# Splitting each large cache load by partitions over two DMA queues

## Chip, core and metric

The kernel runs on one core of one Trainium2 chip. The metric is the device time in microseconds (us); lower is better. Times given for single DMA packets count from the first DMA record of a trace, some 11 us before its span starts; those of profile windows count from the start of the span.

## The reference, cut to what matters

Two attention blocks for one decoded token, side by side. Block A has 32 heads, each with its own cache of 32768 keys and 32768 values of 128 bf16 numbers. Block B is small here (a window of 4096 keys, 8 cache heads).

```python
# block A; block B is the same over a window of 4096 keys
q = (x @ wq).reshape(B, Sq, H, Dh)            # B = Sq = 1, H = 32, Dh = 128
scores = einsum("bhqd,bhkd->bhqk", q, k_cache) * Dh ** -0.5
p = softmax(scores)
o = einsum("bhqk,bhkd->bhqd", p, v_cache)
out = o.reshape(B, Sq, H * Dh) @ wo
```

A head needs 8.4 MB of keys and 8.4 MB of values, each byte once. The whole kernel reads 570 MB.

## The kernel before

SyncE issues every large load. One head's keys are one transfer, its values another: 128 partitions, 64 KB contiguous in each partition. TensorE transposes the keys and multiplies; the key buffer has three thirds of 32 KB per partition, so that the next keys can be loaded while the second half of a head's keys is in use; the value buffer holds one head.

```python
def load(self, dst, src, sem, *deps):
    self.op("sp", lambda e: e.dma_start(dst, src).then_inc(sem, 16), *deps)

def kv_src(self, which, name, g):              # head g, row p = partition p: 64 KB of one head
    ...
    return src.rearrange("s (p j) d -> p s (j d)", p=128)

def load_k(self, g, parts):
    w = HALF * DH                              # 16384 elements, 32 KB: one third of the key buffer
    src = self.kv_src("k", "A", g)[:, 0, :]
    lo = min(self.k_thirds(g))
    free = [self.free["k"][t] for t in self.k_thirds(g)]
    if parts == 1:
        self.load(self.kbuf[:, w * lo:w * lo + 2 * w], src, self.mark("k", 0), *free)
        ...
def load_v(self, g):
    self.load(self.vbuf[:, :], self.kv_src("v", "A", g)[:, 0, :], self.mark("v", 0), *self.free["v"])

# plan(): the main loop, one head per turn
for g in range(NQH):
    self.load_k(g, 1 if g < NQH - 1 else 2)
    self.load_v(g)
    self.emit_qcopy(g)
    self.emit_unit("A", g)        # transposes and scores
    self.emit_stats("A", g)       # maximum, exponential
    self.emit_PT("A", g)
    self.emit_PV("A", g)          # probabilities times values
# ... weights, output projection ...
```

Of the kernel before, what the change touches and what calls it, by code (L numbers as in the profile page):

```python
# [9 lines left out]
DH = 128  # L10
NQH = 32
STRIPS = 4
HALF = 128
NT = 4
# [38 lines left out]
class _Kernel:  # L53
# [176 lines left out]
    def alloc(self):  # L230
        nc = self.nc
        sb = nc.alloc_sbuf_tensor
        self.kbuf = sb("kbuf", [128, 3 * HALF * DH], BF16)
        self.vbuf = sb("vbuf", [128, 2 * HALF * DH], BF16)
        self.kt = [sb(f"kt{i}", [128, 1024], BF16) for i in range(NKT)]
        self.psb = sb("psb", [128, 512], BF16)
        self.ptsb = sb("ptsb", [128, 512], BF16)
        self.ident = sb("ident", [128, 128], BF16)
        self.ones = sb("ones", [128, 128], BF16)
        self.e32 = sb("e32", [128, 32], F32)  # L240
        self.spread = sb("spread", [32, 4, 128], BF16)
        self.tr = {k: sb(f"tr_{k}", [128, 32], F32) for k in ("in", "a")}
        self.rows64 = sb("rows64", [128, 64], F32)
        self.nscale = sb("nscale", [1, 128], F32)
        self.m4 = sb("m4", [1, 128], F32)
        self.pb = sb("pb", [128, 512], F32)
        self.out_sb = sb("out_sb", [128, 512], BF16)
        self.c = {}
        for name, d in self.X.items():
            HG = d["HG"]  # L250
            self.c[name] = dict(
                x=sb(f"x_{name}", [128, 4], BF16),
                oc=[sb(f"oc_{name}{i}", [128, DH + 1], F32) for i in range(2)],
                b=sb(f"b_{name}", [128, 32], F32),
                cm=sb(f"cm_{name}", [128, 32], F32),
                mr=sb(f"mr_{name}", [1, HG], F32),
                nb=sb(f"nb_{name}", [128, 2], F32),
                hot=sb(f"hot_{name}", [128, d["nb"]], F32),
                lh=sb(f"lh_{name}", [128, HG], F32),
                hsel=sb(f"hsel_{name}", [128, 64], F32),  # L260
                rinv=sb(f"rinv_{name}", [32, 1], F32),
                ob=sb(f"ob_{name}", [32, DH], BF16),
                oz=sb(f"oz_{name}", [128, 32], BF16),
            )

        self.qz = sb("qz", [128, 32 * self.X["B"]["NKVH"] + 64], BF16)
        self.qa = sb("qa", [128, NQH], BF16)
        self.qw = sb("qw", [128, 64], BF16)
        self.hw = sb("hw", [128, 32], F32)
        ps = nc.alloc_psum_tensor  # L270
        self.S = ps("psS", [128, 512], F32)
        self.T = [ps(f"psT{i}", [128, 512], F32) for i in range(NT)]
        self.PT = ps("psPT", [128, 512], F32)
        self.ACC = ps("psACC", [128, 512], F32)
        self.G = ps("psG", [128, 512], F32)
        s = nc.alloc_semaphore
        self.ksem = [s(f"ksem{i}") for i in range(2)]
        self.vsem = [s(f"vsem{i}") for i in range(2)]
        self.xsem = {n: s(f"xsem_{n}") for n in self.X}
        self.wosem = {n: [s(f"wosem_{n}{i}") for i in range(len(self.WO_CUTS[n]) - 1)] for n in self.X}  # L280
        self.outsem = {n: s(f"outsem_{n}") for n in self.X}
# [27 lines left out]
    def k_thirds(self, g):  # L309
        return (1, 0) if g % 2 == 0 else (1, 2)  # L310

    def load_k(self, g, parts):
        w = HALF * DH
        src = self.kv_src("k", "A", g)[:, 0, :]
        lo = min(self.k_thirds(g))
        free = [self.free["k"][t] for t in self.k_thirds(g)]
        if parts == 1:
            self.load(self.kbuf[:, w * lo:w * lo + 2 * w], src, self.mark("k", 0), *free)
            sem = self.mark("k", 1)
            self.op("sp", lambda e: e.sem_inc(sem, 16))  # L320
        else:
            for i, t in enumerate(self.k_thirds(g)):
                self.load(self.kbuf[:, w * t:w * t + w], src[:, w * (t - lo):w * (t - lo) + w], self.mark("k", i), *free)

    def load_v(self, g):
        self.load(self.vbuf[:, :], self.kv_src("v", "A", g)[:, 0, :], self.mark("v", 0), *self.free["v"])

    WQ_SLOT = {"B": 0, "A": 1}

# [20 lines left out]
    def plan(self):  # L350
        self.lsem = {"k": self.ksem, "v": self.vsem}
        self.fill = {w: [0, 0] for w in "kv"}
        self.free = {"k": [None] * 3, "v": [None] * 2}
        self.nbatch = 0
        self.copies = []
        self.pending = []
        self.psread = self.ptread = self.sread = self.accread = None
        self.gath = self.qcopy = self.hcopy = None
        self.constants()
        a, b = self.X["A"], self.X["B"]  # L360

        self.load_wq("B")
        self.load_b("k", 0)
        self.load_wq("A")
        self.load_b("k", 1)
        self.emit_qproj("B")
        self.emit_unit("B", 0)
        self.emit_qproj("A")
        self.emit_stats("B", 0)
        self.emit_unit("B", 1, {1: lambda: self.emit_PT("B", 0)})  # L370
        self.emit_stats("B", 1)
        for g in range(2):
            if g == 1:
                self.emit_PT("B", g)
            self.load_b("v", g)
            self.emit_PV("B", g)
        self.emit_spread("B")

        for g in range(NQH):
            self.loop = {"pe": g // 2, "dve": g // 2}  # L380
            self.load_k(g, 1 if g < NQH - 1 else 2)
            self.load_v(g)
            self.emit_qcopy(g)
            self.emit_unit("A", g)
            self.emit_stats("A", g)
            self.emit_PT("A", g)
            self.emit_PV("A", g)
        self.loop = {}
        for n in ("B", "A"):
            for part in range(len(self.WO_CUTS[n]) - 1):  # L390
                self.load_wo(n, part)
        self.emit_spread("A")
        self.emit_proj()
        for n in ("B", "A"):
            self.op("sp", lambda e, n=n: e.wait_ge(self.outsem[n], 16))
# [71 lines left out]
    def emit_unit(self, name, g, hooks={}):  # L467

        d = self.X[name]
        thirds = (g,) if name == "B" else self.k_thirds(g)  # L470
        lo = min(thirds)
        order = [(t, i, 8 * (t - lo) + st) for i, t in enumerate(thirds) for st in range(8)]
        for n, (t, i, st) in enumerate(order):
            for half in range(2):
                self.emit_T(HALF * lo + 16 * st + 8 * half, self.landed("k", g if name == "B" else i), t)
            if n % 2:
                if n // 2 in hooks:
                    hooks[n // 2]()
                self.pending.append((name, g, order[n - 1][2], n == 1, n == len(order) - 1, self.nbatch - 4))
                if len(self.pending) > 1:  # L480
                    self.emit_S(self.pending.pop(0))

    def emit_T(self, tile, landed, third):
        b = self.nbatch
        self.nbatch += 1
        T, KT = self.T[b % NT][:, :].bitcast(BF16), self.kt[b % NKT]
        src = self.kbuf[:, DH * tile:DH * tile + 1024]
        def tr(e):
            inst = None
            for k in range(8):  # L490
                inst = e.transpose(T[:, 128 * k:128 * k + 128], src[:, DH * k:DH * k + DH], self.ident[:, :])  # L491
            return inst
        o = self.op("pe", tr, landed, self.copies[b - NT] if b >= NT else self.k_ident, to="dve")
        self.copies.append(self.op("dve", lambda v: v.tensor_copy(KT[:, :], T[:, :]), o, to="pe"))  # L494
        self.free["k"][third] = o

# [77 lines left out]
    def emit_PV(self, name, g):  # L574
        d, t = self.X[name], self.c[name]
        acc = self.ACC
        pt = self.ptsb[:, :].rearrange("p (j x) -> p j x", x=128)
        if name == "A":
# [3 lines left out]
            rows = 4  # L582
        else:
            w = HALF * DH
# [4 lines left out]
            rows = 16  # L589
        def mm(e):  # L590
# [2 lines left out]
                inst = e.matmul(acc[32 * c:32 * c + rows, 0:512], lhsT=lhsT, rhs=rhs, start=begin, stop=end,  # L593
                                tile_position=(0, 32 * c), skip_group_check=True)
            return inst
        pv = self.op("pe", mm, self.landed("v", 0 if name == "A" else g), self.ptread, self.accread, to="sp")
        for i in (0, 1) if name == "A" else (g,):
            self.free["v"][i] = pv

        pv = self.emit_gather(name, g, DH, DH + 1)  # L600
        oc = t["oc"][g % 2][:, 0:DH]
        o = None
        for j in range(4):
            src, hot = acc[:, DH * j:DH * j + DH], t["hot"][:, j:j + 1]
            to = "pe" if j == 3 else "dve"
            if j == 0:
                o = self.op("dve", lambda v, src=src, hot=hot: v.tensor_scalar_mul(oc, src, hot), pv, self.gath, to=to)  # L607
# [96 lines left out]
```

## Time and profile before

| | before |
|---|---|
| time | 1329.17 us (1329.11 to 1329.23, 2 runs) |
| span of the profiled execution | 1326.8 us |
| read from HBM | 570.43 MB, 430 GB/s over the span |
| 64 KB packets, 5th / 50th / 95th percentile, after the first 160 us | 2.418 / 2.422 / 2.426 us |

The page of the kernel before: busy times, then slices (40 equal parts of the span; for DMA the mean busy tenths of the 16 DMA engines), traffic, the queues, and the chain of work that ended last.

```profile
span 1326.8 us, 28797 instructions
PE 964.5 (73%) x13436; PEld 679.5 (51%) x13436; DVE 749.8 (57%) x1345; ACT 54.8 (4%) x167; POOL 2.3 (0%) x17
...
DMA  9999999999999999999999999999999999999998
GB/s 394 431 431 438 432 433 433 437 429 433 433 435 437 433 435 431 433 433 435 437 433 435 431 433 433 431 441 433 431 435 433 431 433 441 433 431 435 433 431 344
...
q1 hardware_dynamic: 12776, 570.43, 99.6%
...
DMA 70%; PE 28%; DVE 1%; issue 0%; SPq 0%; ACT 0%
```

The DMA engines never rest, and the busiest compute engine, TensorE, works 73% of the time. The q1 line is SyncE's queue: packets, MB, and its share of the time of 16 engines. The chain of waits is 70% DMA. So the kernel is bound by its loads, and its rate hardly leaves room: it is flat at some 433 GB/s from the second slice to the last but one.

The two costliest TensorE groups of the same page, the transposes of the keys and the products with the values (line, engine, operation, tiles, shapes, count; busy us, mean ns of one; idle time before it and who ended it), and three DMA issues (size in KB, median us from issue to landing):

```profile
L491 PE MATMUL psT<-ident,kbuf 128*128 128x128 bf16 x8448 | 579.2, 234 | 176.2 <-DMA kbuf<-in_A_k_cache_dram 164.4
...
L593 PE MATMUL psACC<-vbuf,ptsb 128*4 128x512 bf16 (+1 forms) x2112 | 183.2, 523 | 23.1 <-ACT ptsb L568 21.3
...
vbuf<-in_A_v_cache_dram SPq DMA_DIRECT2D x32, 26.5
...
kbuf<-in_A_k_cache_dram SPq DMA_DIRECT2D x31, 27.8
...
x_B<-in_B_x_dram ACTq DMA_DIRECT2D x1, 1.0 KB, 12.5
```

TensorE waits 164 us for keys, the sign of a load-bound loop. A load lands 26 to 28 us after its issue although its bytes need only 19.35 us (the distance of successive completions), because it is issued early and queues behind the one before. That slack of about 7 us matters for judging issue costs.

### The profile page before, as it was taken

What the parts mean: (1) busy time and instruction counts of PE and PEld (TensorE: products, weight loads), DVE (VectorE), ACT (ScalarE), POOL (GpSimd) and SP (SyncE); (2) the same over time, 40 slices, a digit from 0 to 9 for tenths busy, and PEclk for the clock granted to TensorE, in tenths of its full rate; (3) what the DMA queues carried; (4) which work ended last, traced back from release to release, by engine and by line L of the source; (5) the groups of instructions that cost most, each with busy time, mean ns of one, the idle gap of its engine ahead of it and who ended that gap; (6) DMA issues with size and microseconds to landing.
All of it is one profiled execution on the core that took longest, in us unless ns stands there. A gap on an engine that the chain in (4) does not pass through costs nothing.

```text
span 1326.8 us, 28797 instructions
## 1 busy us (share of the span) xinstructions
PE 964.5 (73%) x13436; PEld 679.5 (51%) x13436; DVE 749.8 (57%) x1345; ACT 54.8 (4%) x167; POOL 2.3 (0%) x17
## 2 busy tenths in 40 slices
PE   3757678777667877766787777678777767877786
PEld 3544455554445555444565544456554445655453
DVE  3645466665456666545666645566654556665473
ACT  0000000000000000000000000000000000000000
POOL 0000000000000000000000000000000000000000
PEclk9877788887788888778888878888887888888798
DMA  9999999999999999999999999999999999999998
GB/s 394 431 431 438 432 433 433 437 429 433 433 435 437 433 435 431 433 433 435 437 433 435 431 433 433 431 441 433 431 435 433 431 433 441 433 431 435 433 431 344
DMA packets 13079, 570.66 MB, mean 430 GB/s; under 512 B 1540, under 2 KB 1544, under 8 KB 1928
## 3 DMA queue, kind: packets, MB, share of 16 engines
q1 hardware_dynamic: 12776, 570.43, 99.6%
q8 instruction: 12, 0.20, 0.1%
q10 hardware_dynamic: 288, 0.00, 0.0%
q14 instruction: 3, 0.02, 0.0%
HBM read 570.43 MB, written 0.00 MB: 430 GB/s over the span
## 4 chain that ended last, share of the span: by engine, by line
DMA 70%; PE 28%; DVE 1%; issue 0%; SPq 0%; ACT 0%
DMA kbuf<-in_A_k_cache_dram 65%; PE psT L491 23%; PE psS L513 4%; DMA kbuf<-in_B_k_cache_dram 3%; DMA kbuf<-in_A_wo_dram 3%; DVE kt L494 1%; PE psACC L593 0%; SPq L286 0%; DVE oc_A L609 0%; ACT psb L541 0%; DVE tr_in L530 0%; PE psPT L565 0%; ACT ptsb L568 0%; PE psPT L655 0%; PE psG L620 0%
## 5 line engine op out<-in xcount | busy, mean ns | idle before, releaser
L494 DVE COPY kt<-psT 128x1024 bf16<-128x1024 bf16 x1056 | 655.2, 684 | 245.0 <-PE psT L491 243.1
L491 PE MATMUL psT<-ident,kbuf 128*128 128x128 bf16 x8448 | 579.2, 234 | 176.2 <-DMA kbuf<-in_A_k_cache_dram 164.4
L491 PEld LDWEIGHTS psT<-ident,kbuf 128*128 128x128 bf16 x8448 | 539.7, 106 | 268.2 <-DMA kbuf<-in_A_k_cache_dram 172.5
L593 PE MATMUL psACC<-vbuf,ptsb 128*4 128x512 bf16 (+1 forms) x2112 | 183.2, 523 | 23.1 <-ACT ptsb L568 21.3
L513 PE MATMUL psS<-kt,qw 128*32 128x512 bf16 x2048 | 157.6, 385 | 15.5 <-DVE kt L494 15.5
L607 DVE TENSOR_SCALAR oc_A<-psACC,hot_A 128x128 f32<-128x128 f32 x32 | 11.2, 351 | 247.8 <-PE psG L620 247.8
L593 PEld LDWEIGHTS psACC<-vbuf,ptsb 128*4 128x4 bf16 (+1 forms) x2112 | 60.0, 110 | 136.9 <-issue 87.2
L541 ACT ACTIVATE psb<-psS,nb_A 128x512 bf16<-128x512 f32 x32 | 22.0, 687 | 1169.9 <-DVE nb_A L540 1169.9
L513 PEld LDWEIGHTS psS<-kt,qw 128*32 128x32 bf16 x2048 | 34.0, 95 | 58.0 <-DVE kt L494 31.4
L620 PE MATMUL psG<-oc_A,hw 128*32 128x128 f32 (+1 forms) x128 | 19.3, 227 | 52.3 <-DVE oc_A L609 52.3
L620 PEld LDWEIGHTS psG<-oc_A,hw 128*32 128x32 f32 x128 | 11.4, 109 | 62.4 <-DVE oc_A L609 55.0
L565 PE MATMUL psPT<-ident,psb 128*128 128x128 bf16 x136 | 17.9, 274 | 34.0 <-ACT psb L541 34.0
L609 DVE SCALAR_TENSOR_TENSOR oc_A<-psACC,hot_A,oc_A 128x128 f32<-128x128 f32 x96 | 33.7, 351 | 3.4
L530 DVE TENSOR_REDUCE tr_in<-psS 128x1 f32<-128x512 f32 x34 | 23.5, 692 | 17.1 <-PE psS L513 17.1
L565 PEld LDWEIGHTS psPT<-ident,psb 128*128 128x128 bf16 x136 | 10.0, 116 | 37.0 <-ACT psb L541 36.7
L534 PE MATMUL psACC<-rows,tr_in 128*1 128x64 f32 x64 | 8.7, 217 | 25.6 <-DVE tr_in L530 25.6
L568 ACT ACTIVATE ptsb<-psPT 128x512 bf16<-128x512 bf16 x34 | 20.3, 597 | 28.2 <-PE psPT L565 28.2
L534 PEld LDWEIGHTS psACC<-rows,tr_in 128*1 128x1 f32 x64 | 2.7, 81 | 35.1 <-DVE tr_in L530 35.1
L538 PE MATMUL psACC<-mr_A,nscale 1*128 1x1 f32 x64 | 12.1, 256 | 9.8 <-DVE mr_A L537 9.8
L538 PEld LDWEIGHTS psACC<-mr_A,nscale 1*128 1x128 f32 x64 | 9.4, 183 | 15.7 <-DVE mr_A L537 15.7
L540 DVE COPY nb_A<-psACC 128x1 f32<-128x1 f32 x32 | 5.1, 158 | 15.0 <-PE psACC L538 15.0
L537 DVE TENSOR_REDUCE mr_A<-psACC 1x1 f32<-1x64 f32 x32 | 6.8, 213 | 11.7 <-PE psACC L534 11.7
(71 smaller groups left out, 75.1 us busy)
## 6 DMA issues: line engine op xcount, KB each, us to landing
kbuf<-in_B_k_cache_dram SPq DMA_DIRECT2D x2, 4096.0 KB, 32.5
vbuf<-in_B_v_cache_dram SPq DMA_DIRECT2D x2, 4096.0 KB, 23.6
kbuf<-in_A_k_cache_dram SPq DMA_DIRECT2D x2, 4096.0 KB, 22.0
vbuf<-in_B_wq_dram SPq DMA_DIRECT2D x1, 4096.0 KB, 12.3
vbuf<-in_A_wq_dram SPq DMA_DIRECT2D x1, 4096.0 KB, 32.4
kbuf<-in_B_wo_dram SPq DMA_DIRECT2D x2, 2048.0 KB, 33.1
kbuf<-in_A_wo_dram SPq DMA_DIRECT2D x1, 1408.0 KB, 28.5
kbuf<-in_A_wo_dram SPq DMA_DIRECT2D x1, 1024.0 KB, 30.6
```

The source lines that it names most:

```text
L491: inst = e.transpose(T[:, 128 * k:128 * k + 128], src[:, DH * k:DH * k + DH], self.ident[:, :])
L494: self.copies.append(self.op("dve", lambda v: v.tensor_copy(KT[:, :], T[:, :]), o, to="pe"))
L513: inst = e.matmul(self.S[32 * c:32 * c + 32, :], lhsT=win, rhs=self.kt[(bb + c // 2) % NKT][:, 512 * (c % 2):512 * (c % 2) + 512], start=b ...
L530: o = dve(lambda v: v.reduce_max(tr["in"][:, 0:1], self.S[:, :], axis=AXX), self.sdone, self.k_pool, to="pe" if name == "A" else None)
L534: o = self.op("pe", lambda e: e.matmul(self.ACC[0:1, 0:64], lhsT=tr["in"][:, 0:1], rhs=self.rows64[:, :], start=True, stop=True, skip_grou ...
L538: o = self.op("pe", lambda e: e.matmul(self.ACC[:, 64:65], lhsT=self.nscale[:, :], rhs=t["mr"][0:1, :], start=True, stop=True, skip_group_ ...
L541: self.sread = self.op("act", lambda s: s.activation(out=self.psb[:, :], in_=self.S[:, :], func=ACTF.Exp, bias=t["nb"][:, k:k + 1], scale= ...
L565: inst = e.transpose(PT[:, 128 * jj:128 * jj + 128], self.psb[:, 128 * jj:128 * jj + 128], self.ident[:, :])
L568: self.ptread = self.op("act", lambda s: s.activation(out=self.ptsb[:, :], in_=PT[:, 0:512], func=ACTF.Copy), self.psread, to="pe")
L593: inst = e.matmul(acc[32 * c:32 * c + rows, 0:512], lhsT=lhsT, rhs=rhs, start=begin, stop=end, tile_position=(0, 32 * c), skip_group_check ...
L609: o = self.op("dve", lambda v, src=src, hot=hot: v.scalar_tensor_tensor(out=oc, in0=src, scalar=hot, in1=oc, op0=ALU.mult, op1=ALU.add), p ...
L620: return self.op("pe", lambda e: e.matmul(self.G[0:32, c0 + c:c0 + c2], lhsT=win, rhs=t["oc"][g % 2][:, c:c2], start=False, stop=True, ski ...
```

## The change

The intent: use a second queue (q10 on the page). Each load of block A becomes two of 64 partitions: 0 to 63 on SyncE's queue, 64 to 127 on ScalarE's. ScalarE waits on a relay semaphore which SyncE raises once it has issued its half, so that the buffer is known to be free.

```diff
-    def load_k(self, g, parts):
+    def load_half(self, queue, which, g, pieces, *deps):
+        src = self.kv_src(which, "A", g)[:, 0, :]
+        rows, n = (slice(0, 64), 0) if queue == "sp" else (slice(64, 128), 1)
+        if queue == "act":
+            deps = [(self.relay[which], g + 1)]
+        for part, dst, a, b in pieces:
+            sem = self.vsem[n] if which == "v" else self.kasem[part][n]
+            self.op(queue, lambda e, ...: e.dma_start(dst[rows, :], src[rows, a:b]).then_inc(sem, 16), *deps)
+        if queue == "sp":
+            self.op("sp", lambda e: e.sem_inc(self.relay[which], 1))
     ...
-    def load_v(self, g):
-        self.load(self.vbuf[:, :], self.kv_src("v", "A", g)[:, 0, :], self.mark("v", 0), *self.free["v"])
+    def load_v(self, queue, g):
+        self.load_half(queue, "v", g, [(0, self.vbuf[:, :], 0, 2 * HALF * DH)], *self.free["v"])
     ...
-            self.load_k(g, 1 if g < NQH - 1 else 2)
-            self.load_v(g)
+            self.load_k("sp", g)
+            self.load_v("sp", g)
     ...   # ScalarE's halves of the next head stand between its own instructions of this head
-        o = self.op("pe", tr, landed, ...)
+        o = self.op("pe", tr, *landed, ...)      # TensorE waits for both halves
```

More of the change, by code (lines that the diff above doesn't have):

```diff
@@ L278, in alloc @@
         self.vsem = [s(f"vsem{i}") for i in range(2)]
+        self.kasem = [[s(f"kasem{i}{j}") for j in range(2)] for i in range(2)]
+        self.relay = {w: s(f"relay_{w}") for w in "kv"}
         self.xsem = {n: s(f"xsem_{n}") for n in self.X}
@@ L310, in k_thirds, with load_k @@
         return (1, 0) if g % 2 == 0 else (1, 2)
-    def load_k(self, g, parts):
+    def load_half(self, queue, which, g, pieces, *deps):
[5 more added lines that the diff above has]
+            sem = self.vsem[n] if which == "v" else self.kasem[part][n]
+            self.op(queue, lambda e, dst=dst, a=a, b=b, sem=sem: e.dma_start(dst[rows, :], src[rows, a:b]).then_inc(sem, 16), *deps)
+        if queue == "sp":
+            self.op("sp", lambda e: e.sem_inc(self.relay[which], 1))
+    def load_k(self, queue, g):
         w = HALF * DH
-        src = self.kv_src("k", "A", g)[:, 0, :]
         lo = min(self.k_thirds(g))
-        free = [self.free["k"][t] for t in self.k_thirds(g)]
-        if parts == 1:
-            self.load(self.kbuf[:, w * lo:w * lo + 2 * w], src, self.mark("k", 0), *free)
-            sem = self.mark("k", 1)
-            self.op("sp", lambda e: e.sem_inc(sem, 16))
-        else:
-            for i, t in enumerate(self.k_thirds(g)):
-                self.load(self.kbuf[:, w * t:w * t + w], src[:, w * (t - lo):w * (t - lo) + w], self.mark("k", i), *free)
-    def load_v(self, g):
-        self.load(self.vbuf[:, :], self.kv_src("v", "A", g)[:, 0, :], self.mark("v", 0), *self.free["v"])
+        if g < NQH - 1:
+            pieces = [(0, self.kbuf[:, w * lo:w * lo + 2 * w], 0, 2 * w)]
+            if queue == "sp":
+                for sem in self.kasem[1]:
+                    self.op("sp", lambda e, sem=sem: e.sem_inc(sem, 16))
+        else:
+            pieces = [(i, self.kbuf[:, w * t:w * t + w], w * (t - lo), w * (t - lo) + w) for i, t in enumerate(self.k_thirds(g))]
+        self.load_half(queue, "k", g, pieces, *[self.free["k"][t] for t in self.k_thirds(g)])
+    def load_v(self, queue, g):
+        self.load_half(queue, "v", g, [(0, self.vbuf[:, :], 0, 2 * HALF * DH)], *self.free["v"])
     WQ_SLOT = {"B": 0, "A": 1}
@@ L380, in plan @@
             self.loop = {"pe": g // 2, "dve": g // 2}
-            self.load_k(g, 1 if g < NQH - 1 else 2)
-            self.load_v(g)
+            self.load_k("sp", g)
+            self.load_v("sp", g)
+            if g == 0:
+                self.load_k("act", g)
+                self.load_v("act", g)
             self.emit_qcopy(g)
             self.emit_unit("A", g)
+            if g < NQH - 1:
+                self.load_k("act", g + 1)
             self.emit_stats("A", g)
@@ L387, in plan @@
             self.emit_PV("A", g)
+            if g < NQH - 1:
+                self.load_v("act", g + 1)
         self.loop = {}
@@ L474, in emit_unit @@
             for half in range(2):
-                self.emit_T(HALF * lo + 16 * st + 8 * half, self.landed("k", g if name == "B" else i), t)
+                self.emit_T(HALF * lo + 16 * st + 8 * half,
+                            [self.landed("k", g)] if name == "B" else [(s, 16 * (g + 1)) for s in self.kasem[i]], t)
             if n % 2:
@@ L492, in tr @@
             return inst
-        o = self.op("pe", tr, landed, self.copies[b - NT] if b >= NT else self.k_ident, to="dve")
+        o = self.op("pe", tr, *landed, self.copies[b - NT] if b >= NT else self.k_ident, to="dve")
         self.copies.append(self.op("dve", lambda v: v.tensor_copy(KT[:, :], T[:, :]), o, to="pe"))
@@ L595, in mm @@
             return inst
-        pv = self.op("pe", mm, self.landed("v", 0 if name == "A" else g), self.ptread, self.accread, to="sp")
+        landed = [self.landed("v", g)] if name == "B" else [(s, 16 * (g + 3)) for s in self.vsem]
+        pv = self.op("pe", mm, *landed, self.ptread, self.accread, to="sp")
         for i in (0, 1) if name == "A" else (g,):
```

## The prediction

The sum ("full collision") takes each load at twice its measured 19.35 us, an assumption of mine: 64 x 38.7 + 91 = 2568 us. The factor 0.9 for lags between the engines (about 2400) was my estimate. A further case: 1330 to 2000 us; the forecast was 2350 us, range 1500 to 2600.

> **What bounds the kernel now.** The loads. The page gives 570.66 MB at 430 GB/s over a span of 1326.8 us, DMA busy 9 tenths in every slice but the last, and one queue (SyncE's) with 99.6% of the 16 engines' time. The chain of waits is 70% DMA, 65% of it on the A keys. TensorE is 73% busy, but before each head's transposes it sits idle for the keys (164.4 us in all). The trace's DMA records show 8064 packets of 64 KB (one row of one partition), each 2.42 us long, 27 GB/s per engine, with hardly a spread. Completions of successive loads are 19.35 us apart: 64 loads x 19.35 = 1238 us; the other 91 us are B's loads, start and end. So only some 1% could be won even by a perfect stream.
>
> **What the change does.** Bytes and arithmetic stay. Each 128x64 KB load becomes two of 64 rows: rows 0-63 from SyncE, 64-127 from ScalarE, released through a relay semaphore. Issue cost is 0.33 us each, about 64 more on ScalarE, which is 4% busy. Loads are issued early: keys take 27.8 us from issue to landing and values 26.5, against 19.35 of transfer, so about 7 us of queueing hides the relay and ScalarE's waits. The tensor engine gets a second semaphore to wait on per load. I put all this at under 3 us on the critical path.
>
> **Where I expect the loss.** Which SBUF side the rows reach.[...] No run here shows that yet.
>
> With two queues an engine alternates. In this trace the small x loads on ScalarE's queue advance one descriptor per 32 KB packet of SyncE's queue (every 1.215 us), so an engine serves one descriptor at a time, turn about.[...] Completions of one load lie within 3.3 us over the engines[...].
>
> Full collision: 64 x 38.7 + 91 = 2568 us. With lags leaving 0.9 of it: about 2400.[...]
>
> **Predicted: 2350 us, range 1500 to 2600; faster 2%, within 2% 18%, slower 80%.**
>
> **What would show it.** Right: 64 KB packets much longer than 2.42 us (up to 4.84); GB/s of 220-260 in the middle slices; DMA still busy; both queues near half of the bytes; TensorE waiting longer for keys and values; issue to landing near 50 us. Wrong: packets still 2.42 us and 430 GB/s with two queues[...]; or DMA idle in the middle slices with short packets (then ScalarE's late issue is the cause[...]).
>
> **What would make it wrong.** [...]an engine interleaving the two queues more finely than a descriptor[...]: then 1325 to 1345 us.

## The result, and the profile after

| | before | after |
|---|---|---|
| time | 1329.17 us | 2435.43 us (2418.74 to 2452.11, 2 runs) |
| ratio | | 1.832, 95% interval 1.803 to 1.862 |
| 64 KB packets, 5th / 50th / 95th percentile | 2.418 / 2.422 / 2.426 us | 3.555 / 4.758 / 5.089 us |

Ratios here and below are the mean time of one kernel's runs over that of the kernel before's in the same rounds, so not quite the ratio of the medians quoted. Executions over 1.5% slower than the fastest of the same kernel are left out of the means. Bytes are the same: 570.43 MB.

The same parts of the page for the kernel after:

```profile
span 2450.1 us, 29036 instructions
PE 972.4 (40%) x13436; PEld 684.8 (28%) x13436; DVE 749.4 (31%) x1345; ACT 58.4 (2%) x167; POOL 2.3 (0%) x17
...
DMA  9999999999999999999999999999999999999997
GB/s 404 223 217 214 217 214 216 214 216 219 213 216 220 214 220 223 220 226 236 233 241 246 249 243 247 261 242 221 234 243 255 218 223 229 232 234 239 233 231 218
...
q1 hardware_dynamic: 8616, 302.00, 51.6%
q10 hardware_dynamic: 5488, 268.44, 48.1%
...
L511 PE MATMUL psT<-ident,kbuf 128*128 128x128 bf16 x8448 | 578.7, 234 | 939.0 <-DMA kbuf<-in_A_k_cache_dram 926.5
...
L613 PE MATMUL psACC<-vbuf,ptsb 128*4 128x512 bf16 (+1 forms) x2112 | 189.4, 536 | 364.0 <-DMA vbuf<-in_A_v_cache_dram 360.4
...
vbuf<-in_A_v_cache_dram SPq DMA_DIRECT2D x32, 63.3
vbuf<-in_A_v_cache_dram ACTq DMA_DIRECT2D x32, 67.4
```

The DMA engines are still busy in nearly every slice, and yet they move half as much: 213 to 261 GB/s after the first slice. They are not waiting for work; each packet lasts longer. The work of the transposes on TensorE is unchanged (578.7 us against 579.2), and nearly all the added time is waiting for keys (926.5 us against 164.4) and for values (360.4 us, where before that group idled 23.1 us in all). The profile could not follow this kernel's chain that ended last, so the reading rests on the waits and on the packets.

A sum from the packets: 8064 packets of 64 KB over 16 engines are 504 each; 504 x 4.598 us (their mean over the whole run) = 2317 us, and the 91 us outside the cache loads make 2408, against a span of 2450; the other 42 us were not looked into.

The trace's DMA records carry the queue of each packet, its start and its length. They give one more fact. At moments between 200 and 1000 us when 8 or 9 of the 16 packets in flight go to one half of the partitions and the rest to the other, the rate is still 219 GB/s; when 15 or 16 go to the same half it is 209 to 211. And the 16 packets in flight all last nearly the same: their standard deviation averages 30 to 90 ns at a mean of 4.76 to 5.02 us. The clearest case: from 223.44 to 228.53 us a single packet goes to the lower half while all the 15 others go to the upper one. It has its half to itself, and it still lasts 5.09 us. Twenty more before 1000 us are alone in their half for 3.0 to 3.4 us and last 4.87 to 5.01 us. That does not fit my reason for the loss (cut above), by which a packet alone in its half should have been as fast as before, and the experiments return to it.

### The profile page after: what moved, and what is told of

It reads as the page before. It is cut to its first block, busy times and chain, and to the rows that moved or that the text cites. A ratio compares the mean times of both kernels' runs of the same rounds, so it can differ in the third digit from the quotient of the medians.

```text
span 2450.1 us, 29036 instructions
## 1 busy us (share of the span) xinstructions
PE 972.4 (40%) x13436; PEld 684.8 (28%) x13436; DVE 749.4 (31%) x1345; ACT 58.4 (2%) x167; POOL 2.3 (0%) x17
## 3 DMA queue, kind: packets, MB, share of 16 engines
HBM read 570.43 MB, written 0.00 MB: 233 GB/s over the span
## 5 line engine op out<-in xcount | busy, mean ns | idle before, releaser
L511 PE MATMUL psT<-ident,kbuf 128*128 128x128 bf16 x8448 | 578.7, 234 | 939.0 <-DMA kbuf<-in_A_k_cache_dram 926.5
L613 PE MATMUL psACC<-vbuf,ptsb 128*4 128x512 bf16 (+1 forms) x2112 | 189.4, 536 | 364.0 <-DMA vbuf<-in_A_v_cache_dram 360.4
L483 ACT ACTIVATE qw<-qa 128x1 bf16<-128x1 bf16 x32 | 6.6, 206 | 539.5 <-SPq L323 539.5
```

The costliest lines, as they stand in the source:

```text
L511: inst = e.transpose(T[:, 128 * k:128 * k + 128], src[:, DH * k:DH * k + DH], self.ident[:, :])
L613: inst = e.matmul(acc[32 * c:32 * c + rows, 0:512], lhsT=lhsT, rhs=rhs, start=begin, stop=end, tile_position=(0, 32 * c), skip_group_check ...
```

## The experiments

The main theory: the destination decides. A load into 64 neighbouring partitions of one half of SBUF (0 to 63 or 64 to 127 of the 128 partitions of the kernel's buffers) is slow, whatever the queue. My reason why was shown by no run. The expectations: the first figures in each are those of the main theory, the later ones those of its rivals, unless the text below it says otherwise. Rivals: (1) two queues on the same engines cost time by themselves; (2) ScalarE issues late or the relay stalls; (3) any split or smaller transfer is slow; (4) the HBM addresses clash; (5) one half is slow by itself for the engines that write it. Three groups of kernels tell them apart. The windows shown are from 600 to 700 us: busy us (and instructions) of PE (TensorE), PEld (its weight loads), DVE (VectorE), ACT (ScalarE) and POOL (GpSimd), then TensorE's granted clock, the DMA share, and GB/s. For comparison, this line of before and then of after:

```profile
600.00:700.00 100.00, 74.48 (x1030) 51.01 (x1026) 57.20 (x102) 4.76 (x15) 0.00 (x0) 0.85 1.00 434
```

```profile
600.00:700.00 100.00, 34.97 (x464) 22.14 (x460) 24.18 (x44) 3.19 (x9) 0.00 (x0) 0.66 1.01 217
```

### Two queues, or the partitions?

**Split by columns** (two queues, the relay and ScalarE's issues kept):

```diff
-        rows, n = (slice(0, 64), 0) if queue == "sp" else (slice(64, 128), 1)
+        n = 0 if queue == "sp" else 1
+            h = (b - a) // 2
-            ... e.dma_start(dst[rows, :], src[rows, a:b]) ...
+            ... e.dma_start(dst[:, h * n:h * n + h], src[:, a + h * n:a + h * n + h]) ...
```

> Two queues, same relay and same ScalarE issues, but every load is split by columns, so each half spans all 128 partitions. [...]packets of 32 KB at 1.21 us, GB/s about 430 in the middle, 1325 to 1345 us. Rival 1 (two queues on one engine cost time) and rival 2 (ScalarE's late issue, the relay): about 2435 us as in the change, with packets of 32 KB near 2.3 us (rival 1) or idle DMA (rival 2).

Measured: 1335.53 us, ratio 1.0045 (1.0029 to 1.0062), right result. Packets of 32 KB lasted 1.218 us in the median. Two queues, the relay and ScalarE's place in the program cost half a per cent together. Rivals 1 and 2 fall.

**Split by partitions, one queue**:

```diff
-        if queue == "act":
-            deps = [(self.relay[which], g + 1)]
+        if queue == "act":
+            return
+            for n, rows in enumerate((slice(0, 64), slice(64, 128))):
+                ... self.op("sp", ... e.dma_start(dst[rows, :], src[rows, a:b]) ...)
```

> The partition split is kept, but both halves are issued on SyncE, one after the other; no relay. [...]the lag of at most 3.3 us between engines is small against the 9.7 us of four rows, so nearly full collision: 2350 to 2570 us, packets 4.6 to 4.9 us. Rival 1 and rival 2 (two queues, late issue): 1325 to 1345 us, packets 2.42 us.

Measured: 2666.11 us, ratio 2.007 (2.004 to 2.011). Packets 5.01 us in the mean, longer than foreseen; by the sum above (504 x 5.01 + 91 = 2616 us) that is most of why the time lies above the expected range. With one queue the split costs even more than with two.

**Whole loads on two queues** (keys on SyncE, values on ScalarE):

```diff
+        rows, n = slice(0, 128), 0
+            if queue == ("act" if which == "v" else "sp"):
+                ... e.dma_start(dst[rows, :], src[rows, a:b]) ...
```

> Two queues, no split: the keys as whole 128-partition loads on SyncE, the values as whole loads on ScalarE behind the same relay. [...]packets of 64 KB at 2.42 us, 1325 to 1345 us. Two queues as such to blame: about 2435 us.

Measured: 1354.84 us, ratio 1.0193 (1.0175 to 1.0210), just above the range expected. Packets 2.443 us in the mean; the slices show one of 340 and several of 407 to 420 GB/s where before has 429 or more. These two per cent were not pursued; they are not the change's 83%.

### Which partitions?

**Only partitions 0 to 63, and only 32 to 95** (the kernel before, one queue; from the third head on half of the bytes, so the result is wrong; same size and same count of transfers):

```diff
+    def load_rows(self, g, dst, src, sem, *deps):
+        rows = slice(0, 128) if g < 2 else slice(0, 64)       # second kernel: slice(32, 96)
+        self.load(dst[rows, :], src[rows, :], sem, *deps)
```

> The kernel before, one queue, but from the third head on each cache load fetches only partitions 0 to 63 (wrong result on purpose: half of the bytes). [...]packets of 64 KB at 4.84 us, a load of 4.2 MB still takes 19.4 us, GB/s about 217, time about as before, 1290 to 1340 us. Every rival that blames the second queue or the splitting: packets 2.42 us, loads of 9.7 us, the tensor engine becomes the limit: before's 1329 less its 164 us of waiting for keys, 1120 to 1190 us.

> As the run with partitions 0 to 63 only, but partitions 32 to 95 (wrong result on purpose, the same half of the bytes). [...]packets 2.42 us, loads 9.7 us, tensor engine limits, 1120 to 1190 us. If any load of 64 partitions is slow by its size or split alone: like the run with 0 to 63, 1290 to 1340 us.[...]

Measured: 0 to 63 takes 1394.57 us, ratio 1.049 (1.048 to 1.051); half of the bytes takes longer than all of them. The time lies above the first range expected, since a packet took 5.1 us and not 4.84 (twice 2.42). 32 to 95 takes 1142.25 us, ratio 0.860 (0.858 to 0.861). Their windows, first 0 to 63, then 32 to 95:

```profile
600.00:700.00 100.00, 66.35 (x888) 46.48 (x889) 47.86 (x84) 4.53 (x15) 0.00 (x0) 0.81 0.99 204
```

```profile
600.00:700.00 100.00, 81.37 (x1200) 55.14 (x1204) 65.06 (x117) 6.34 (x20) 0.00 (x0) 0.92 0.61 252
```

In the first the engines are busy all the time at 204 GB/s, with packets of 5.116 us (median). In the second they are idle for 39% of the time, so the loads are no longer the limit, and a packet lasts 2.420 us (median; of those over 2.6 us, up to 3.9, all but one start after a pause). So neither the number of 64 partitions nor the size of a transfer is slow. It depends on which 64. Rival 3 falls.

**Bytes of rows 0 to 63 into partitions 32 to 95** (wrong):

```diff
+        self.load(dst[32:96, :], src[0:64, :], sem, *deps)     # from the third head on
```

> As the run with partitions 32 to 95 only, but the bytes come from rows 0 to 63 of HBM (wrong result on purpose), so the source is that of the slow run and the destination that of the fast one. If the destination partitions decide: packets 2.42 us, about 1142 us. If the HBM addresses decide: packets 5.1 us, about 1395 us.

Measured: 1141.83 us, ratio 0.859 (0.858 to 0.861), packets 2.420 us in the median. The destination decides, not the HBM addresses. Rival 4 falls.

**Even partitions on SyncE, odd ones on ScalarE** (the change with one line edited, right result):

```diff
-        rows, n = (slice(0, 64), 0) if queue == "sp" else (slice(64, 128), 1)
+        rows, n = (slice(0, 127, 2), 0) if queue == "sp" else (slice(1, 128, 2), 1)
```

> The change as it is, two queues, but SyncE takes the even partitions and ScalarE the odd ones[...]. [...]no loss, 1325 to 1345 us, packets 2.42 us. [...]packets near 5 us, 2450 to 2680 us.

Measured: 1329.90 us, ratio 1.0005 (0.9988 to 1.0022). Packets 2.420 us in the median. Its window:

```profile
600.00:700.00 100.00, 76.08 (x1063) 51.55 (x1060) 58.45 (x104) 4.89 (x14) 0.00 (x0) 0.85 1.00 432
```

The same split into two halves by partitions, on the same two queues with the same relay, costs nothing measurable if the parts take every other partition (ratio 1.0005). The second figures of the expectation (packets near 5 us) rested on an assumed assignment of rows to engines and did not come; how the rows went to the engines here is not known. The split also gains nothing: no version with a right result tried here beats the kernel before.

**Eight packets in flight, on either half** (wrong; from the third head on keys into 0 to 63 only, values into 64 to 127 only, each as 8 transfers of 8 rows, 4 partitions apart):

```diff
+        half = 0 if which == "k" else 64
+        for a in range(8):
+            p = half + 32 * (a // 4) + a % 4
+            rows = slice(p, p + 29, 4)
+            self.load(dst[rows, :], src[rows, :], self.mark(which, i), *deps)
```

> From the third head on the keys load only partitions 0 to 63 and the values only 64 to 127 (wrong result on purpose), each as 8 transfers of 8 rows, 4 partitions apart[...]. [...]all packets 2.42 us for keys and values alike, 8 in flight, loads of 19.4 us, GB/s about 215, 1320 to 1380 us. [...]packets of one of the two halves near 4.8 us, loads of 19.4 and 38.7 us in turn, 1900 to 2000 us.

(The first figures are those if neither half is slow by itself, the second those if one of them is.)

Measured: 1350.19 us, ratio 1.016 (1.014 to 1.018). Its window:

```profile
600.00:700.00 100.00, 74.21 (x1031) 50.86 (x1028) 57.16 (x102) 4.76 (x15) 0.00 (x0) 0.85 0.50 216
```

Between 300 and 1000 us 8 packets are in flight in 99% of the samples, and packets last 2.418 us, keys and values alike. (Transfers are issued while earlier ones still run, and never are more than 8 packets in flight; which engines carry them the trace does not name.) So with 8 packets in flight into one half, either half takes them in the 2.42 us of the kernel before. Rival 5 falls for the engines at work here. Note the price: 8 packets in flight into 64 partitions of one half move 216 GB/s, and 16 no more (204).

One rival was not put to a run of its own: that half of SBUF takes some 216 GB/s as a whole. The trace of the change speaks against it. From 2182 to 2202 us the packets in flight stay spread over both halves (5 to 11 in each, 8 in the mean). By an estimate from these numbers, 8 packets of 64 KB need 2.4 us at 216 GB/s; the 54 packets within that time lasted 4.48 to 4.84 us. So a limit of 216 GB/s per half does not account for them.

### Packets in flight that last alike

**Partitions 16 to 79 only** (as above, wrong):

```diff
-        rows = slice(0, 128) if g < 2 else slice(0, 64)
+        rows = slice(0, 128) if g < 2 else slice(16, 80)
```

> As the run with partitions 0 to 63 only, but partitions 16 to 79 (wrong result on purpose, half of the bytes). [...]two kinds of 64 KB packets, 2.42 and about 5.1 us, in equal numbers; the load still waits for the slow ones, 1330 to 1400 us. [...]all packets near 5.1 us with a spread of some 0.1 us, 1380 to 1400 us as in the run with 0 to 63.[...]

Measured: 1392.36 us, ratio 1.046 (1.042 to 1.049). Packets 5.028 / 5.066 / 5.122 us (5th, 50th, 95th percentile), and none of the 3747 below 4.3 us. Its window:

```profile
600.00:700.00 100.00, 67.90 (x916) 48.61 (x908) 51.24 (x90) 3.18 (x10) 0.00 (x0) 0.80 1.00 208
```

The first figures of the expectation were for two kinds of packets, some slow and some at 2.42 us; the second for all packets slow, and those came: though 16 of the 64 partitions lie in the other half, every packet is about as slow as with 0 to 63 (5.116 us in the median). So it is not enough that a load has partitions in both halves. Why the fast ones are missing was not shown; my reason rested on an assumed assignment of rows to engines, which the trace does not name. What stands is measured: here the packets last alike (5.028 to 5.122 us), and the packet in the change that was alone in its half lasted 5.09 us.

**Does the engines' lag matter?** Two kernels let ScalarE's queue join at the third head, and the second also puts one transfer of eight 32 KB packets ahead of the first head ("step theory" was my idea that a lag between engines shortens packets):

```diff
+        if g < 2:
+            if queue == "act":
+                return
+            rows = slice(0, 128)             # the first two heads whole, on SyncE
+            ...
 # second kernel, ahead of the first head (kbuf's last third is free then):
+        self.op("sp", lambda e: e.dma_start(self.kbuf[0:32:4, 2 * w:3 * w], ksrc[0:32:4, 0:w]) ...)
```

> The change, but the first two heads are loaded whole on SyncE; ScalarE's queue joins at the third head. Then 64 KB packets are in flight when it joins[...]. Step theory: packets of the first split loads are spread[...], so 3.0 to 5.1 us[...]; total 2100 to 2500 us. If the lag does not matter[...]: packets 4.8 to 5.1 us from the third head on and the change's time less two heads' loss (about 80 us), 2340 to 2390 us.

> As the run that joins at the third head, with one more transfer ahead of the first head: 8 rows of 32 KB[...] into a part of the key buffer that is free then.[...] the packets of the first split loads differ from the run without it by about that: if lags were near zero, from about 4.9 to about 3.7 us (GB/s near 280 in the first split loads). If the lag does not matter: same as without it.

Measured: 2498.49 us, ratio 1.883 (1.879 to 1.887), and 2452.30 us, ratio 1.842 (1.834 to 1.849), each from three fast executions. The eight 32 KB packets stand in the second trace, at 73 to 75 us, 1.21 to 1.23 us each. Packets that start between 150 and 160 us, in the first split loads, last 5.18 and 5.04 us (medians). So joining later, and the eight packets ahead, did not bring the packets down; what I expected of lags is not seen. (Whether the eight packets still set any engine back when ScalarE's queue joined, the trace does not show, as it does not name engines.) The first of the two is also slower than the change, by some 2.6%, not faster; why is open. The second does not differ from the change beyond the spread of the runs.

**Middle half and two outer quarters** (right result, one queue):

```diff
-            for n, rows in enumerate((slice(0, 64), slice(64, 128))):
+            for n, rows in ((0, slice(32, 96)), (1, slice(0, 32)), (1, slice(96, 128))):
```

> All loads on SyncE, each split by partitions into three: 32 to 95, then 0 to 31, then 96 to 127; all bytes, right result. [...]30.1 us per load, 64 x 30.1 + 91 = about 2020 us, range 1950 to 2080, and two kinds of packets, near 2.42 and near 5.1 us. If any partition split on one queue costs like the one at 64: about 2666 us; if only the size of the parts matters, more than that.

(The 30.1 us per load are 4 packets of 2.42 us for the middle part, as in the run with 32 to 95, and 2 + 2 of 5.11 us for the outer ones, as in the run with 0 to 63; that the outer parts are slow was assumed.)

Measured: 2460.76 us, ratio 1.854 (1.849 to 1.860), a miss by 440 us. The two kinds of packets are there (3.1 thousand of 7.7 thousand below 3.2 us, most others from 4.4 to 5.6 us), but the engines are idle for part of the time:

```profile
600.00:700.00 100.00, 42.38 (x591) 32.00 (x591) 34.22 (x59) 1.59 (x5) 0.00 (x0) 0.68 0.79 206
```

The DMA share is 0.79. In one load looked at in the trace, starting at 600 us, most engines had finished by 625 us, a few went on until 634 with packets of up to 7.2 us, and the others started the next load only at 633. My sum took the engines to stay together. What makes some of them fall behind was not settled, so this run says little about the theory. It does show that packets in flight together need not last alike: at 627 us packets of 7.1 and 7.2 us were in flight beside one of 2.42 us.

## Why the prediction was right or wrong

The time lay inside the range: 2435 us measured, 2350 predicted, 1500 to 2600 allowed. Point by point:

- **"So only some 1% could be won even by a perfect stream": right.** The even/odd split, with two queues and packets of 2.420 us, measured 1.0005.
- **Issue costs "under 3 us on the critical path": somewhat small, and not the cause.** The column split carries all of them and took 6.6 us longer (1335.53 against 1328.97), a difference that also holds the smaller packets.
- **"Which SBUF side the rows reach": right as far as shown, by elimination.** Partitions 0 to 63 alone gave packets of 5.116 us, 32 to 95 alone and the even/odd split 2.420 us. The source addresses, the queues, the relay and a half that is slow by itself were each taken out. Why the destination decides was not shown.
- **The step from there to the packet time failed.** By it a packet is slow only while others go to the same half. In the change a packet that had its half to itself for all of its time still lasted 5.09 us instead of 2.42. At moments with the packets split evenly between the halves the change still moved 219 GB/s, all 16 packets in flight last nearly the same, and with partitions 16 to 79 no packet of 3747 was below 4.3 us. Why they last alike, and why the three-part split shows packets of 7.1 and 7.2 us beside one of 2.42, no run shows.
- **The sizes.** A slow packet was taken as 2 x 2.42 = 4.84 us. Alone on one queue it measured 5.1 us (0 to 63), and the one-queue split 2666 us, above my "full collision" of 2568. In the change the mean was 4.60 us. The prediction came near for a partly wrong reason, and so partly by luck: it took 0.9 of full collision for the effect of lags, which the runs do not show. Why two queues are 230 us better than one is open; the change's packets do get shorter in places, from 4.88 us in the first fifth to 4.27 between 1300 and 1700 us, and no experiment explained that.
- **What was named as the sign of a miss** (packets of 2.42 us, or idle DMA) did not appear, and the signs of a hit did, with three sizes somewhat off: packets up to 5.09 us (95th percentile) instead of 4.84, slices from 213 GB/s instead of 220, and 57 to 67 us from issue to landing instead of 50.

## What to carry to other kernels

When the DMA engines are already busy all the time, a second queue has nothing to give (here 99.6% busy before; ratios of 1.0005 to 1.0193 with two queues where the packets stayed near their old rate). If a load must be split, the splits that cost nothing or little here were by columns (1.0045) and by even and odd partitions (1.0005); a part of 64 neighbouring partitions in one half of SBUF ran at half the rate here (204 GB/s for 0 to 63), 16 to 79 did no better (208), and 32 to 95 kept packets of 2.420 us. Busy DMA is no proof of speed: look at GB/s and at the length of one packet of known size.
